# A block-sparse attention and two MLPs on one core: the second MLP's input combinations are made a block ahead, kept in DRAM, and split 768 columns wide

## The chip, the cores and the metric

The kernel runs on one core of a Trainium2 chip. The metric is device time in microseconds (us) of one execution, lower is better. Five engines work side by side, each in the order of its own instructions: PE (matmuls, TensorE), DVE (VectorE), ACT (ScalarE), POOL (GpSimd) and SP (which only issues DMAs here). They wait for each other on semaphores.

## The reference

```python
# attention, 4 batches, 8 heads, 576 positions, 64 channels a head, mask by blocks of 64
scores = where(mask, scale * q @ k.T, -1e9)
x = (softmax(scores) @ v)            # as [2304 tokens, 512 channels]
# first MLP: 512 -> 2048 -> 512
h = x @ w_in;  g = s * relu(h)**2 + b;  x = g @ w_out
# second MLP: 512 -> 2048 -> 512
h = x @ w2_in; g = maximum(0.01 * h, h); out = g @ w2_out
```

All is fp32. The weights come as 64-bit words, which the kernel decodes itself.

## The kernel before

**fp32 out of two halves.** PE multiplies fp32 values rounded to a shorter form (`float32r`). So that nothing is lost, each operand is split: a high part `hi` (a cast on ScalarE) and a low part `lo = x - hi` (a subtraction on VectorE). Each product is three matmuls, hi x hi, hi x lo and lo x hi.

**The first MLP** goes through the tokens in five blocks, with the attention of the next block worked in between. Its result goes channel by token to the DRAM tensor `yT` (line 936), without the constant `c` that b adds; `c_sb` holds c, known only after the fourth block (line 932), and is added when the values are read back. In the first MLP's last stretch the kernel also prepares the second MLP's weights in sixteen "units", each in a tile of the pool `stg` (2 tiles, 16 KB a partition): twelve first, four more (`units(1, ...)`, line 944) in the last block.

**The second MLP** uses a Strassen-Winograd scheme: seven products (`PRODUCTS`, line 387) of 2 x 2 blocks take the place of eight. The tokens go in three blocks `j` of 768 columns, two halves of `NH` = 384; the 2048 hidden channels in two halves. That makes six steps, `STEPS` = (block, half) = (0,0), (0,1), (1,1), (1,0), (2,0), (2,1) on line 962. A step has an input phase, 4 pairs `i` of 7 products (`in_pair`, line 1072, 28 in all), and an output phase, 7 products of 4 pairs each (`out_phase`, line 1113, 28 in all). Every product is six matmuls of 384 columns, on line 1090 or 1156. In both phases the products come in the order `IN_ORDER` = 1, 5, 6, 3, 7, 2, 4. The output phase needs for each of its products a high and a low part of hidden values (`gh2`, 3 tiles, line 1149; `gl2`, 2 tiles, line 1150), VectorE's combinations of the tiles `G` (16 tiles, four a pair), and additions to the results `Y` (4 tiles, line 1168). The second step of a block stores Y to the output.

**The block's input**, `x_load(j)` (line 1011): the four quarters of x (two halves of channels by two halves of tokens, `x11` to `x22`) are read from yT, for the channel chunks c = 0 and c = 1 in turn, as tiles of 384 columns (line 1025); ScalarE adds c (line 1030); VectorE makes the combinations T1 to T4 of Winograd's scheme in place (`comb`, line 1046); and each of the seven operands is split, high part on line 1040, low part on line 1041 (VectorE's subtractions all have line 1003, that of the helper `sub`). The pool `X` has 29 tiles of 384 columns: 28 hold the parts of the current block, so a new block's quarters wait for parts that the last input products give back. A block is used by two steps, and x_load runs three times: at the end of the first MLP, and in the output phases of steps 1 and 3.

**The order of the work** is made by a planner (class `Graph`, line 44). Every piece of work is a step with an engine, an estimated duration, the steps it waits for (`after`), the tiles that it opens and uses, and a due time. `order()` (line 87) plays the schedule through: an engine that is idle takes the ready step with the earliest due time whose tiles are free. A due time only ranks; a step runs early if nothing else is ready. Pools in `inturn` (line 261: stg, X, Y, gl2 and others) give tiles in the order of due times. DMAs are planned one after the other at 300 GB/s. The steps are then emitted in that order, and each engine keeps it. A `gate` (line 77) closes one group of pools and opens another in the same memory once all users of the old one have been placed: `xin` (pool X) takes the attention's place, `mlp2` (pools w2, gh2, gl2, Y, G) that of the first MLP.

**Weights of the second MLP** are loaded a step ahead by `load_units` (line 967): eight input units `wi` (two a pair, 0.92 MB each) and seven output weights `wo` (1.05 MB each), each placed behind the one before (`behind=line[-1:]`). Before, wi and the first four wo sit in the 12 tiles of pool `w`, which the first MLP's weights give back one after the other, and the last three wo in the 3 tiles of `w2`.

Of the kernel before, what the change touches and what calls it, by code (L numbers as in the profile page):

```python
# [8 lines left out]
F32 = mybir.dt.float32  # L9
# [182 lines left out]
NB = 5  # L192
# [4 lines left out]
def kernel(  # L197
# [48 lines left out]
    def close_pools(group):  # L246
        for p in reversed(opened.pop(group)):
            p.release()

    MLP1 = (("stg", 2), ("gh", 2), ("gl", 2), ("g", 1), ("st", 2), ("xh", 4), ("xl", 4))  # L250
    ATT = (("xf", 4), ("k", 2), ("kh", 1), ("kl", 1), ("q", 3), ("qs", 1), ("v", 3), ("p", 2), ("pt", 3), ("sm", 6))
    MLP2 = (("w2", 3), ("gh2", 3), ("gl2", 2), ("Y", 4), ("G", 16))
    XIN = (("X", 29),)
    open_pools("mlp1", "left", MLP1)
    open_pools("att", "right", ATT)
    pools.update({
# [17 lines left out]
    s_sb = const.tile([128, 1], F32, name="s_sb")  # L274
    b_sb = const.tile([128, 1], F32, name="b_sb")
    yT = dr_p.tile([DM, NT], F32, name="yT")
    kept = dr_p.tile([2 * KEEP, 128, 2048], F32, name="kept")
    u_in = dr_p.tile([NF, 128, 2, 896], F32, name="u_in")
    u_out = dr_p.tile([2, 7, 128, 8, 2, 128], F32, name="u_out")
# [675 lines left out]


    G.gate(lambda e: (close_pools("att"), open_pools("xin", "right", XIN)), [k for k, _ in ATT], [k for k, _ in XIN])
    G.gate(lambda e: (close_pools("mlp1"), open_pools("mlp2", "left", MLP2)), [k for k, _ in MLP1], [k for k, _ in MLP2])

    ONE = 6 * (NH / 2400 + 0.013)  # L960
    IN_ORDER = (1, 5, 6, 3, 7, 2, 4)
# [5 lines left out]
    def load_units(n):  # L967

        j, half = STEPS[n]
        if n and STEPS[n - 1][1] == half:  # L970
            for m in (in_w, in_ok):
                for i in range(4):
                    for c in range(2):
                        m[n, i, c] = m[n - 1, i, c]
            for m in (out_w, out_ok):
                for r in range(1, 8):
                    m[n, r] = m[n - 1, r]
            return
        k = 0

        def gate():
            nonlocal k
            k += 1
            return [done[NB - 1, min(NF - 1, KEEP + max(k - 1, -KEEP))]] if n == 0 else []

        for i in range(4):
            for c in range(2):
                w = in_w[n, i, c] = buf("w", [128, 2, 7, 128], F32R, "wi")
                in_ok[n, i, c] = G.add(
                    {"SP": 0.65}, lambda e, w=w, u=8 * half + 2 * i + c: e.dma_start(  # L990
                        out=w().bitcast(F32).rearrange("p s r n -> p s (r n)"), in_=u_in[u]),
                    [*unit_ok[half, 0, i], *gate()], [w], [], t2[n] + 7 * ONE * i - 14, nbytes=917504, behind=line[-1:])
                line.append(in_ok[n, i, c])
        for o, r in enumerate(IN_ORDER):
            w = out_w[n, r] = buf("w2" if r in (7, 2, 4) else "w", [128, 8, 2, 128], F32R, "wo")
            x = OUT7.index(PRODUCTS[r][0])
            out_ok[n, r] = G.add(
                {"SP": 0.65}, lambda e, w=w, half=half, x=x: e.dma_start(out=w().bitcast(F32), in_=u_out[half, x]),
                [*[s for i in range(4) for s in unit_ok[half, 1, i]], *gate()], [w], [], t2[n] + 28 * ONE + 4 * ONE * o - 14, nbytes=1048576, behind=line[-1:])
            line.append(out_ok[n, r])  # L1000
# [5 lines left out]
        return {"DVE": dve(n)}  # L1006

    x2 = {}
    in_last = [None]

    def x_load(j):

        n0 = [n for n, s in enumerate(STEPS) if s[0] == j][0]
        t = t2[n0] - 24
        x2.update({(j, r, c): [buf("X", [128, NH], F32R, "xh2"), buf("X", [128, NH], F32R, "xl2"), None] for r in PRODUCTS for c in range(2)})
        for c in range(2):
            raw, ok = {}, {}
            for a in (1, 2):
                for b in (1, 2):
                    raw[a, b] = buf("X", [128, NH], F32, "xr")  # L1020
                    row, col = (2 * (a - 1) + c) * 128, 2 * NH * j + NH * (b - 1)
                    from_ = [y_st[k, 2 * (a - 1) + c] for k in range(NB) if T0[k] < col + NH and T0[k] + TB[k] > col]
                    t += 0.01
                    ld = G.add(
                        {"SP": 0.65}, lambda e, x=raw[a, b], row=row, col=col: e.dma_start(out=x(), in_=yT[row:row + 128, col:col + NH]),
                        [*from_, in_last[0]], [raw[a, b]], [], t - 4, nbytes=512 * NH)

                    def add_c(e, x=raw[a, b], cc=c_sb[:, 2 * (a - 1) + c:2 * (a - 1) + c + 1]):
                        if e is nc.scalar:
                            e.activation(out=x(), in_=x(), func=ACTF.Identity, bias=cc)  # L1030
                        else:
                            e.tensor_scalar(out=x(), in0=x(), scalar1=cc, scalar2=None, op0=ALU.add)

                    ok[a, b] = G.add({"ACT": act(NH) + 0.05}, add_c, [ld, *c_ok], [], [raw[a, b]], t, port=True)

            def split(r, x, after):
                nonlocal t
                t += 0.6
                hi, lo, _ = x2[j, r, c]
                a = G.add({"ACT": act(NH)}, lambda e: e.activation(out=hi(), in_=x(), func=ACTF.Copy), after, [hi], [x], t)  # L1040
                a = G.add({"DVE": dve(NH)}, lambda e: sub(e, lo(), x(), hi().bitcast(F32)), [a], [lo], [hi, x], t, port=True)
                x2[j, r, c][2] = a
                return a

            def comb(x, y, z, after):
                return G.add(tt(NH), lambda e: sub(e, x(), y(), z()), after, [], [x, y, z], t, port=True)

            x11, x12, x21, x22 = raw[1, 1], raw[1, 2], raw[2, 1], raw[2, 2]
            a = split(1, x11, [ok[1, 1]])
            t1 = comb(x11, x12, x11, [a, ok[1, 2]])  # L1050
            a = split(5, x11, [t1])
            tt2 = comb(x11, x22, x11, [a, ok[2, 2]])
            split(6, x11, [tt2])
            a = split(2, x21, [ok[2, 1]])
            t4 = comb(x21, x21, x11, [a, tt2])
            t3 = comb(x12, x22, x12, [t1, ok[2, 2]])
            split(7, x12, [t3])
            split(4, x21, [t4])
            split(3, x22, [ok[2, 2]])

    gt = {}

# [9 lines left out]
    def in_pair(n, i):  # L1072
# [8 lines left out]
        for o, r in enumerate(IN_ORDER):  # L1081
            due = t + o * ONE
            x, first = where[r]
            ai = IN7.index(PRODUCTS[r][0])

            def fn(e, r=r, x=x, first=first, ai=ai):
                for c in range(2):
                    hi, lo, _ = x2[j, r, c]
                    for m, (s, y) in enumerate(((0, hi), (0, lo), (1, hi))):
                        e.matmul(out=x()[:, :NH], lhsT=in_w[n, i, c]()[:, s, ai], rhs=y(), start=(first and c == 0 and m == 0), stop=(c == 1 and m == 2),  # L1090
                                 skip_group_check=True)

            after = [*[in_ok[n, i, c] for c in range(2)], *[x2[j, r, c][2] for c in range(2)]]
            after += {6: [ev.get(1)], 7: [ev.get(6)], 4: [ev.get(7)], 3: [ev.get(5)]}.get(r, [])
            p = G.add({"PE": ONE}, fn, after, [x] * first, [x, *[in_w[n, i, c] for c in range(2)], *[q for c in range(2) for q in x2[j, r, c][:2]]], due)
            in_last[0] = p
            d2 = due + ONE
            if r in (1, 5, 6):
                y = g[{1: (1, 1), 5: (2, 2), 6: (1, 2)}[r]]
                ev[r] = G.add({"ACT": act(NH)}, lambda e, x=x, y=y: copy(e, y(), x()[:, :NH]), [p], [y], [x], d2)  # L1100
            elif r in (2, 3, 7):
                y = g[{2: (1, 1), 3: (1, 2), 7: (2, 2)}[r]]
                ev[r] = a = G.add({"DVE": dve(NH)}, lambda e, x=x, y=y: add(e, y(), x()[:, :NH]), [p, ev[{2: 1, 3: 6, 7: 5}[r]]], [], [x, y], d2)
                ok[{2: (1, 1), 3: (1, 2), 7: (2, 2)}[r]] = G.add(
                    {"ACT": act(NH)}, lambda e, y=y: e.activation(out=y(), in_=y(), func=ACTF.Lrelu), [a], [], [y], d2 + 2)  # L1105
            else:
                y = g[2, 1]
                ok[2, 1] = G.add({"ACT": act(NH)}, lambda e, x=x, y=y: e.activation(out=y(), in_=x()[:, :NH], func=ACTF.Lrelu), [p], [y], [x], d2)
# [81 lines left out]
    for n in range(len(STEPS)):  # L1190
        if n == 0 or STEPS[n][0] != STEPS[n - 1][0]:
            x_load(STEPS[n][0])
        load_units(n)
        for i in range(4):
            in_pair(n, i)
        out_phase(n)
# [53 lines left out]
```

## Time and profile before

| | |
|---|---|
| median of 3 runs | 967.18 us (963.68 to 967.64) |
| the profiled execution | 969.23 us |
| its span, first to last instruction | 967.2 us |
| PE busy | 940.6 us, 97% |
| VectorE busy | 655.7 us, 68% |
| ScalarE busy | 579.3 us, 60% |
| GpSimd busy | 103.6 us, 11% |
| DMA | 197.26 MB, mean 204 GB/s |

The span lies inside the execution; some 2 us lie around it. Busy times are shares of the whole span; stages differ, and a hole in PE's row counts only where it is. Matmuls overlap in the records: a matmul of 384 columns lasts 335 ns there, while the next one starts some 174 ns after it.

### The profile page before, as it was taken

To read this page: it belongs to the slowest core of one execution; us is meant where nothing else is said; L and a number is where in the kernel's file an instruction comes from. 1 tells how busy PE (TensorE), PEld (TensorE's weight loads), DVE (VectorE), ACT (ScalarE), POOL (GpSimd) and SP (SyncE) were. 2 spreads that over 40 slices of the span, in tenths; PEclk is the share of its full clock that TensorE was granted. 3 is DMA by queue.
4 is the path that set the end of the run, shared out by engine and by line. 5 is a ranking of instruction groups with operands and counts; after the bars stand their busy time and mean duration, and the time that the engine had idled before them with its cause. 6 is when DMAs were issued, how large, how long until landed. Compare 5 with 4: busy or idle time off the path is not lost. (4 is left out here: it accounts for less than half of the span.)

```text
span 967.2 us, 16689 instructions
## 1 busy us (share of the span) xinstructions
PE 940.6 (97%) x5780; PEld 826.7 (85%) x5780; DVE 655.7 (68%) x1342; ACT 579.3 (60%) x1247; POOL 103.6 (11%) x232
## 2 busy tenths in 40 slices
PE   9799999999998999999999999999989999899998
PEld 8678887777776787888887888999989999799998
DVE  5798877777786776676677752556595565955657
ACT  4678666676676566666676632555565555645443
POOL 1112321111121212112221000000000000000000
PEclk9999999999999999999999999999999999999999
DMA  8896277985768987466346996973115741157402
GB/s 221 289 335 205 69 249 258 319 260 194 215 202 244 312 276 246 154 217 189 99 141 186 353 350 218 387 291 139 58 37 199 289 160 57 33 188 288 168 1 66
DMA packets 143828, 197.26 MB, mean 204 GB/s; under 512 B 23296, under 2 KB 118144, under 8 KB 137088
## 3 DMA queue, kind: packets, MB, share of 16 engines
q1 hardware_dynamic: 141296, 195.41, 61.4%
q10 hardware_dynamic: 2448, 0.79, 0.4%
q8 instruction: 46, 0.75, 0.3%
q14 instruction: 38, 0.31, 0.1%
HBM read 148.96 MB, written 47.19 MB: 203 GB/s over the span
## 5 line engine op out<-in xcount | busy, mean ns | idle before, releaser
L874 PE MATMUL h<-xh,w 128*128 128x512 f32 (+1 forms) x640 | 231.7, 392 | 2.6 <-ACT g L890 0.8
L917 PE MATMUL y<-gh,w 128*128 128x512 f32 (+1 forms) x640 | 186.2, 374 | 0.0
L874 PEld LDWEIGHTS h<-xh,w 128*128 128x128 f32 x640 | 118.9, 190 | 30.5 <-issue 5.3
L917 PEld LDWEIGHTS y<-gh,w 128*128 128x128 f32 x640 | 114.6, 188 | 20.8 <-issue 1.1
L1149 ACT ACTIVATE gh<-G 128x384 fp32r<-128x384 f32 x168 | 86.8, 524 | 59.3 <-PE A L1156 25.4
L1003 DVE TENSOR_TENSOR gl<-G,gh 128x384 fp32r<-128x384 f32 x168 | 92.6, 555 | 43.3 <-PE A L1156 18.7
L874 PE MATMUL h<-xl,w 128*128 128x512 f32 (+1 forms) x320 | 118.9, 372 | 1.0 <-DVE xl L857 1.0
L917 PE MATMUL y<-gl,w 128*128 128x512 f32 (+1 forms) x320 | 118.6, 371 | 1.1 <-DVE gl L893 1.0
L1090 PE MATMUL A<-xh,wi 128*128 128x384 f32 x384 | 112.3, 335 | 0.3 <-ACT G L1065 0.2
L1156 PE MATMUL A<-gh,wo 128*128 128x384 f32 x384 | 98.4, 337 | 1.5 <-ACT gh L1149 1.5
L890 ACT ACTIVATE g<-h 128x512 f32<-128x512 f32 (+1 forms) x80 | 44.4, 555 | 71.1 <-PE h L874 63.1
L1090 PEld LDWEIGHTS A<-xh,wi 128*128 128x128 f32 x384 | 70.6, 188 | 1.0 <-ACT G L1065 1.0
L1156 PEld LDWEIGHTS A<-gh,wo 128*128 128x128 f32 x384 | 69.1, 188 | 2.8 <-ACT gh L1149 2.1
L563 PE MATMUL t<-id_sb,p 128*128 128x128 f32 x400 | 66.0, 279 | 5.3 <-DVE p L533 3.1
L917 PEld LDWEIGHTS y<-gl,w 128*128 128x128 f32 x320 | 60.2, 188 | 12.3 <-DVE gl L893 2.0
L1105 ACT ACTIVATE G<-G 128x384 f32<-128x384 f32 x72 | 37.8, 525 | 51.5 <-DVE G L1070 51.4
L479 ACT ACTIVATE pt<-t 128x512 f32<-128x512 f32 (+2 forms) x84 | 44.3, 530 | 39.5 <-PE t L563 38.2
L563 PEld LDWEIGHTS t<-id_sb,p 128*128 128x128 f32 x400 | 47.9, 141 | 22.6 <-issue 7.1
L874 PEld LDWEIGHTS h<-xl,w 128*128 128x128 f32 x320 | 60.9, 190 | 7.3 <-DVE xl L857 1.3
L1156 PE MATMUL A<-gl,wo 128*128 128x384 f32 x192 | 64.7, 337 | 0.3
L1090 PE MATMUL A<-xl,wi 128*128 128x384 f32 x192 | 64.3, 335 | 0.0
L893 DVE TENSOR_TENSOR gl<-g,gh 128x512 fp32r<-128x512 f32 (+1 forms) x80 | 51.4, 643 | 16.5 <-ACT gh L892 14.1
(124 smaller groups left out, 1859.6 us busy)
## 6 DMA issues: line engine op xcount, KB each, us to landing
wi<-u_in SPq DMA_DIRECT2D x32, 896.0 KB, 6.2
wo<-u_out SPq DMA_DIRECT2D x28, 1024.0 KB, 5.7
w<-kept SPq DMA_DIRECT2D x16, 1024.0 KB, 7.0
u_in<-unit SPq DMA_DIRECT2D x16, 896.0 KB, 5.1
u_out<-unit SPq DMA_DIRECT2D x32, 448.0 KB, 5.4
early<-in_moe_w_in_dram SPq DMA_DIRECT2D x16, 512.0 KB, 6.0
early<-in_moe_w_out_dram SPq DMA_DIRECT2D x16, 512.0 KB, 6.7
kept<-w SPq DMA_DIRECT2D x8, 1024.0 KB, 8.0
```

Source lines behind the costliest of these rows:

```text
L479: e.activation(out=out, in_=in_, func=ACTF.Copy, scale=by)
L563: e.transpose(tb()[:, x * 128:(x + 1) * 128], P()[:, pc:pc + 128], id_sb)
L874: e.matmul(out=h()[:, :T], lhsT=w()[:, wi, c * 128:(c + 1) * 128], rhs=x[blk, c]()[:, :T], start=(c == 0 and n == 0), stop=(c == KD - 1 an ...
L890: a = G.add({"ACT": act(T)}, lambda e: e.activation(out=g()[:, :T], in_=h()[:, :T], func=ACTF.Relu), [prev], [g], [h], due)
L893: lo = G.add({"DVE": dve(T)}, lambda e: e.tensor_tensor(out=gl()[:, :T], in0=g()[:, :T], in1=gh()[:, :T].bitcast(F32), op=ALU.subtract), [ ...
L917: e.matmul(out=y()[:, :W], lhsT=w()[:, wi, d * 128:(d + 1) * 128], rhs=x()[:, :W], start=(pos == 0 and n == 0), stop=(pos == NF - 1 and n ...
L1003: e.tensor_tensor(out=out, in0=x, in1=y, op=ALU.subtract)
L1090: e.matmul(out=x()[:, :NH], lhsT=in_w[n, i, c]()[:, s, ai], rhs=y(), start=(first and c == 0 and m == 0), stop=(c == 1 and m == 2), skip_g ...
L1105: {"ACT": act(NH)}, lambda e, y=y: e.activation(out=y(), in_=y(), func=ACTF.Lrelu), [a], [], [y], d2 + 2)
L1149: hi = G.add({"ACT": act(NH)}, lambda e, gh=gh, x=x: e.activation(out=gh(), in_=x(), func=ACTF.Copy), [a], [gh], [x], due - 2)
L1156: e.matmul(out=z[d]()[:, :NH], lhsT=out_w[n, r]()[:, 2 * i + d, s], rhs=y(), start=(first and i == 0 and m == 0), stop=(i == 3 and m == 2) ...
```

## The change

- The input combinations of blocks 1 and 2 are made by a new function `x_stage`, ahead of `x_load`: quarters of both channel chunks are read at once (tiles of 768 columns, `x_raw`), c is added on ScalarE, 384 columns at a time, T1 to T4 are made 768 columns wide, and all seven operands are stored to a new DRAM tensor `x_dr` as fp32. For block 1 this runs in one tile of `stg`, with due times in the last block of the first MLP; for block 2 in the four tiles of `Y`, with due times in step 2.
- `x_load(1)` and `x_load(2)` only read the seven operands and split them, 768 columns an instruction (`x_part`). Loads no longer wait for the last input product (`in_last` is gone); they wait for the store and for a tile of X.
- Block 0 (`x_first`) still goes from yT to its parts in one go, 768 columns wide.
- X has 15 tiles of 768 columns in place of 29 of 384. `gl2` has 3 tiles in place of 2.
- Input units 5, 6 and 7 use `w2`, and all seven output weights use `w`.

The diff, without the old body of x_load, which stands above:

```diff
--- before.py
+++ after.py
@@ -249,8 +249,8 @@
 
     MLP1 = (("stg", 2), ("gh", 2), ("gl", 2), ("g", 1), ("st", 2), ("xh", 4), ("xl", 4))
     ATT = (("xf", 4), ("k", 2), ("kh", 1), ("kl", 1), ("q", 3), ("qs", 1), ("v", 3), ("p", 2), ("pt", 3), ("sm", 6))
-    MLP2 = (("w2", 3), ("gh2", 3), ("gl2", 2), ("Y", 4), ("G", 16))
-    XIN = (("X", 29),)
+    MLP2 = (("w2", 3), ("gh2", 3), ("gl2", 3), ("Y", 4), ("G", 16))
+    XIN = (("X", 15),)
     open_pools("mlp1", "left", MLP1)
     open_pools("att", "right", ATT)
     pools.update({
@@ -274,6 +274,7 @@
     s_sb = const.tile([128, 1], F32, name="s_sb")
     b_sb = const.tile([128, 1], F32, name="b_sb")
     yT = dr_p.tile([DM, NT], F32, name="yT")
+    x_dr = dr_p.tile([2, 7, 128, 2, NH], F32, name="x_dr")
     kept = dr_p.tile([2 * KEEP, 128, 2048], F32, name="kept")
     u_in = dr_p.tile([NF, 128, 2, 896], F32, name="u_in")
     u_out = dr_p.tile([2, 7, 128, 8, 2, 128], F32, name="u_out")
@@ -955,7 +956,6 @@
 
 
     G.gate(lambda e: (close_pools("att"), open_pools("xin", "right", XIN)), [k for k, _ in ATT], [k for k, _ in XIN])
-    G.gate(lambda e: (close_pools("mlp1"), open_pools("mlp2", "left", MLP2)), [k for k, _ in MLP1], [k for k, _ in MLP2])
 
     ONE = 6 * (NH / 2400 + 0.013)
     IN_ORDER = (1, 5, 6, 3, 7, 2, 4)
@@ -985,14 +985,14 @@
 
         for i in range(4):
             for c in range(2):
-                w = in_w[n, i, c] = buf("w", [128, 2, 7, 128], F32R, "wi")
+                w = in_w[n, i, c] = buf("w2" if 2 * i + c > 4 else "w", [128, 2, 7, 128], F32R, "wi")
                 in_ok[n, i, c] = G.add(
                     {"SP": 0.65}, lambda e, w=w, u=8 * half + 2 * i + c: e.dma_start(
                         out=w().bitcast(F32).rearrange("p s r n -> p s (r n)"), in_=u_in[u]),
                     [*unit_ok[half, 0, i], *gate()], [w], [], t2[n] + 7 * ONE * i - 14, nbytes=917504, behind=line[-1:])
                 line.append(in_ok[n, i, c])
         for o, r in enumerate(IN_ORDER):
-            w = out_w[n, r] = buf("w2" if r in (7, 2, 4) else "w", [128, 8, 2, 128], F32R, "wo")
+            w = out_w[n, r] = buf("w", [128, 8, 2, 128], F32R, "wo")
             x = OUT7.index(PRODUCTS[r][0])
             out_ok[n, r] = G.add(
                 {"SP": 0.65}, lambda e, w=w, half=half, x=x: e.dma_start(out=w().bitcast(F32), in_=u_out[half, x]),
@@ -1006,57 +1006,106 @@
         return {"DVE": dve(n)}
 
     x2 = {}
-    in_last = [None]
+
+    class View:
+
+        def __init__(self, buf, view=lambda x: x):
+            self.buf, self.view = buf, view
+
+        def __call__(self):
+            return self.view(self.buf())
+
+    def x_part(j, r, x, after, t):
+
+        hi, lo, _ = x2[j, r]
+        a = G.add({"ACT": act(2 * NH)}, lambda e: e.activation(out=hi(), in_=x(), func=ACTF.Copy), after, [hi], [x.buf], t)
+        x2[j, r][2] = a = G.add({"DVE": dve(2 * NH)}, lambda e: sub(e, lo(), x(), hi().bitcast(F32)), [a], [lo], [hi, x.buf], t, port=True)
+        return a
+
+    def x_raw(j, key, t, name):
+
+        raw, ok = {}, {}
+        whole = buf("stg", [128, 2, 2, 1024], F32, name) if key == "stg" else None
+        for y, (a, b) in enumerate(((1, 1), (1, 2), (2, 2), (2, 1))):
+            if whole is None:
+                x = View(buf(key, [128, 2, NH], F32, name))
+            else:
+                x = View(whole, lambda w, y=y: w[:, y // 2, y % 2, :2 * NH].rearrange("p (c n) -> p c n", c=2))
+            raw[a, b] = x
+            row, col = 2 * (a - 1) * 128, 2 * NH * j + NH * (b - 1)
+            from_ = [y_st[k, 2 * (a - 1) + c] for k in range(NB) for c in range(2) if T0[k] < col + NH and T0[k] + TB[k] > col]
+            t += 0.01
+            ld = G.add(
+                {"SP": 0.65}, lambda e, x=x, row=row, col=col: e.dma_start(
+                    out=x(), in_=yT[row:row + 256, col:col + NH].rearrange("(c p) n -> p c n", c=2)),
+                from_, [x.buf] if whole is None or not y else [], [x.buf], t, nbytes=1024 * NH)
+            ok[a, b] = [
+                G.add({"ACT": act(NH) + 0.05}, lambda e, x=x, c=c, cc=c_sb[:, 2 * (a - 1) + c:2 * (a - 1) + c + 1]: e.activation(
+                    out=x()[:, c], in_=x()[:, c], func=ACTF.Identity, bias=cc), [ld, *c_ok], [], [x.buf], t + 4)
+                for c in range(2)
+            ]
+        return raw, ok
+
+    def x_comb(x, y, z, after, t):
+        return G.add(tt(2 * NH), lambda e: sub(e, x(), y(), z()), after, [], [x.buf, y.buf, z.buf], t, port=True)
+
+    def x_first():
+
+        t = t2[0] - 24
+        for r in PRODUCTS:
+            x2[0, r] = [buf("X", [128, 2, NH], F32R, "xh2"), buf("X", [128, 2, NH], F32R, "xl2"), None]
+        raw, ok = x_raw(0, "X", t - 4, "xr")
+        x11, x12, x21, x22 = raw[1, 1], raw[1, 2], raw[2, 1], raw[2, 2]
+        a = x_part(0, 1, x11, ok[1, 1], t)
+        t1 = x_comb(x11, x12, x11, [a, *ok[1, 2]], t + 1)
+        a = x_part(0, 5, x11, [t1], t + 2)
+        tt2 = x_comb(x11, x22, x11, [a, *ok[2, 2]], t + 3)
+        x_part(0, 6, x11, [tt2], t + 4)
+        t3 = x_comb(x12, x22, x12, [t1, *ok[2, 2]], t + 5)
+        x_part(0, 7, x12, [t3], t + 6)
+        a = x_part(0, 2, x21, ok[2, 1], t + 7)
+        t4 = x_comb(x21, x21, x11, [a, tt2], t + 8)
+        x_part(0, 4, x21, [t4], t + 9)
+        x_part(0, 3, x22, ok[2, 2], t + 10)
+
+    x_st = {}
+
+    def x_stage(j, key, t):
+
+        raw, ok = x_raw(j, key, t, "xs")
+        x11, x12, x21, x22 = raw[1, 1], raw[1, 2], raw[2, 1], raw[2, 2]
+
+        def store(r, x, after):
+            a = x_st[j, r] = G.add({"SP": 0.65}, lambda e: e.dma_start(out=x_dr[j - 1, r - 1], in_=x()), after, [], [x.buf], t + 6, nbytes=1024 * NH)
+            return a
+
+        s1 = store(1, x11, ok[1, 1])
+        t1 = x_comb(x12, x12, x11, [*ok[1, 1], *ok[1, 2]], t + 6)
+        s5 = store(5, x12, [t1])
+        s3 = store(3, x22, ok[2, 2])
+        tt2 = x_comb(x12, x22, x12, [s5, *ok[2, 2]], t + 6)
+        store(6, x12, [tt2])
+        t3 = x_comb(x11, x12, x11, [s1, tt2], t + 6)
+        store(7, x11, [t3])
+        s2 = store(2, x21, ok[2, 1])
+        t4 = x_comb(x21, x21, x12, [s2, tt2], t + 6)
+        store(4, x21, [t4])
 
     def x_load(j):
 
+        if not j:
+            x_first()
+            return
         n0 = [n for n, s in enumerate(STEPS) if s[0] == j][0]
         t = t2[n0] - 24
-        x2.update({(j, r, c): [buf("X", [128, NH], F32R, "xh2"), buf("X", [128, NH], F32R, "xl2"), None] for r in PRODUCTS for c in range(2)})
...
+        for o, r in enumerate(IN_ORDER):
+            x2[j, r] = [buf("X", [128, 2, NH], F32R, "xh2"), buf("X", [128, 2, NH], F32R, "xl2"), None]
+            x = View(buf("X", [128, 2, NH], F32, "xr"))
+            ld = G.add({"SP": 0.65}, lambda e, r=r, x=x: e.dma_start(out=x(), in_=x_dr[j - 1, r - 1]), [x_st[j, r]], [x.buf], [], t - 4 + 0.1 * o, nbytes=1024 * NH)
+            x_part(j, r, x, [ld], t + o)
+
+    x_stage(1, "stg", begin[NB - 1] + 4)
+    G.gate(lambda e: (close_pools("mlp1"), open_pools("mlp2", "left", MLP2)), [k for k, _ in MLP1], [k for k, _ in MLP2])
 
     gt = {}
 
@@ -1085,15 +1134,14 @@
 
             def fn(e, r=r, x=x, first=first, ai=ai):
                 for c in range(2):
-                    hi, lo, _ = x2[j, r, c]
+                    hi, lo, _ = x2[j, r]
                     for m, (s, y) in enumerate(((0, hi), (0, lo), (1, hi))):
-                        e.matmul(out=x()[:, :NH], lhsT=in_w[n, i, c]()[:, s, ai], rhs=y(), start=(first and c == 0 and m == 0), stop=(c == 1 and m == 2),
+                        e.matmul(out=x()[:, :NH], lhsT=in_w[n, i, c]()[:, s, ai], rhs=y()[:, c], start=(first and c == 0 and m == 0), stop=(c == 1 and m == 2),
                                  skip_group_check=True)
 
-            after = [*[in_ok[n, i, c] for c in range(2)], *[x2[j, r, c][2] for c in range(2)]]
+            after = [*[in_ok[n, i, c] for c in range(2)], x2[j, r][2]]
             after += {6: [ev.get(1)], 7: [ev.get(6)], 4: [ev.get(7)], 3: [ev.get(5)]}.get(r, [])
-            p = G.add({"PE": ONE}, fn, after, [x] * first, [x, *[in_w[n, i, c] for c in range(2)], *[q for c in range(2) for q in x2[j, r, c][:2]]], due)
-            in_last[0] = p
+            p = G.add({"PE": ONE}, fn, after, [x] * first, [x, *[in_w[n, i, c] for c in range(2)], *x2[j, r][:2]], due)
             d2 = due + ONE
             if r in (1, 5, 6):
                 y = g[{1: (1, 1), 5: (2, 2), 6: (1, 2)}[r]]
@@ -1191,6 +1239,8 @@
         if n == 0 or STEPS[n][0] != STEPS[n - 1][0]:
             x_load(STEPS[n][0])
         load_units(n)
+        if n == 2:
+            x_stage(2, "Y", t2[n] + 2)
         for i in range(4):
             in_pair(n, i)
         out_phase(n)
```

## Rows read from the trace of the kernel before

**Rows 1.** The page: its first part (busy us, share of the span, instructions) and the granted clock.

```profile
PE 940.6 (97%) x5780; PEld 826.7 (85%) x5780; DVE 655.7 (68%) x1342; ACT 579.3 (60%) x1247; POOL 103.6 (11%) x232
...
PEclk9999999999999999999999999999999999999999
```

**Rows 2.** Stretches: length, busy us (count) of PE, PEld, DVE, ACT, POOL; clock, DMA, GB/s.

```profile
600.00:620.00 20.00, 19.69 (x108) 18.57 (x107) 10.06 (x18) 11.55 (x22) 0.00 (x0) 1.00 0.95 365
680.00:700.00 20.00, 19.64 (x112) 19.09 (x111) 11.50 (x22) 11.81 (x26) 0.00 (x0) 1.00 0.22 70
680.00:740.00 60.00, 56.21 (x315) 54.05 (x314) 44.77 (x90) 35.48 (x75) 0.00 (x0) 1.00 0.24 81
692.93:724.65 31.72, 27.93 (x151) 25.77 (x151) 29.27 (x62) 22.26 (x47) 0.00 (x0) 1.00 0.09 26
740.00:800.00 60.00, 60.00 (x348) 60.00 (x347) 34.08 (x65) 31.35 (x66) 0.00 (x0) 1.00 0.59 218
800.00:860.00 60.00, 56.23 (x315) 54.07 (x314) 43.10 (x87) 35.61 (x75) 0.00 (x0) 1.00 0.25 80
940.00:960.00 20.00, 19.64 (x112) 19.09 (x111) 17.14 (x36) 9.55 (x19) 0.00 (x0) 1.00 0.15 40
```

**Rows 3.** The chain that ended last: start, us, line, matmuls.

```profile
853.29 1.04 PE A L1090 x6
```

**Rows 4.** PE's timeline: start, us, line, tiles, count, idle time ahead and its releaser.

```profile
521.34 0.50 PE L874 MATMUL h<-xh,w 128*128 128x512 f32 x1 [0.76 <-DVE g L888]
...
603.31 0.39 PE L917 MATMUL y<-gl,w 128*128 128x512 f32 x1
...
611.75 0.51 PE L1156 MATMUL A<-gh,wo 128*128 128x384 f32 x2
...
685.65 0.33 PE L1090 MATMUL A<-xh,wi 128*128 128x384 f32 x1
...
691.89 0.34 PE L1090 MATMUL A<-xh,wi 128*128 128x384 f32 x1
...
707.98 0.44 PE L1156 MATMUL C<-gl,wo 128*128 128x384 f32 x1 [1.54 <-DVE gl L1003]
...
720.71 0.44 PE L1156 MATMUL B<-gl,wo 128*128 128x384 f32 x1 [0.98 <-DVE gl L1003]
```

**Rows 5.** VectorE's timeline in the first block switch.

```profile
706.91 0.55 DVE L1003 TENSOR_TENSOR xl<-xr,xh 128x384 fp32r<-128x384 f32 x1
707.38 0.55 DVE L1003 TENSOR_TENSOR gl<-G,gh 128x384 fp32r<-128x384 f32 x1
```

**Rows 6.** Groups by line and shape: busy us, mean ns | idle ahead, releasers.

```profile
L893 DVE TENSOR_TENSOR gl<-g,gh 128x512 fp32r<-128x512 f32 x64 | 44.1, 690 | 16.5 <-ACT gh L892 14.1 <-PE y L917 2.1
...
L1003 DVE TENSOR_TENSOR xl<-xr,xh 128x384 fp32r<-128x384 f32 x42 | 22.7, 551 | 4.6 <-ACT xh L1040 4.6
...
L334 DVE TENSOR_TENSOR w<-early,w 128x1024 fp32r<-128x1024 f32 x15 | 18.3, 1218 | 1.2 <-ACT w L331 1.2
...
L1040 ACT ACTIVATE xh<-xr 128x384 fp32r<-128x384 f32 x42 | 20.3, 512 | 3.3 <-DVE xr L1003 3.3
...
L1030 ACT ACTIVATE xr<-xr,c_sb 128x384 f32<-128x384 f32 x24 | 13.3, 604 | 0.7 <-DMA xr<-yT 0.7
```

**Rows 7.** ScalarE's timeline at the first switch.

```profile
696.52 2.12 ACT L1030 ACTIVATE xr<-xr,c_sb 128x384 f32<-128x384 f32 x4
```

**Rows 8.** DMA issues: KB each, median us from issue to landing.

```profile
xr<-yT SPq DMA_DIRECT2D x24, 192.0 KB, 3.7
```

**Rows 9.** SP's timeline: DMA issues at the first MLP's end.

```profile
529.20 3.72 SPq L417 DMA_DIRECT2D unit<-in_moe_w_out_dram  x1
...
572.41 1.57 SPq L458 DMA_DIRECT2D u_out<-unit  x2
...
605.07 2.43 SPq L998 DMA_DIRECT2D wo<-u_out  x3
```

More of the change, by code (lines that the diff above doesn't have):

```diff
@@ L1011, in x_load @@
     def x_load(j):
+        if not j:
+            x_first()
+            return
         n0 = [n for n, s in enumerate(STEPS) if s[0] == j][0]
         t = t2[n0] - 24
-        x2.update({(j, r, c): [buf("X", [128, NH], F32R, "xh2"), buf("X", [128, NH], F32R, "xl2"), None] for r in PRODUCTS for c in range(2)})
[L1016 to L1038, printed above, removed]
-                hi, lo, _ = x2[j, r, c]
[L1040 to L1059, printed above, removed]
@@ L1087, in fn @@
                 for c in range(2):
-                    hi, lo, _ = x2[j, r, c]
+                    hi, lo, _ = x2[j, r]
                     for m, (s, y) in enumerate(((0, hi), (0, lo), (1, hi))):
-                        e.matmul(out=x()[:, :NH], lhsT=in_w[n, i, c]()[:, s, ai], rhs=y(), start=(first and c == 0 and m == 0), stop=(c == 1 and m == 2),
+                        e.matmul(out=x()[:, :NH], lhsT=in_w[n, i, c]()[:, s, ai], rhs=y()[:, c], start=(first and c == 0 and m == 0), stop=(c == 1 and m == 2),
                                  skip_group_check=True)
-            after = [*[in_ok[n, i, c] for c in range(2)], *[x2[j, r, c][2] for c in range(2)]]
+            after = [*[in_ok[n, i, c] for c in range(2)], x2[j, r][2]]
             after += {6: [ev.get(1)], 7: [ev.get(6)], 4: [ev.get(7)], 3: [ev.get(5)]}.get(r, [])
-            p = G.add({"PE": ONE}, fn, after, [x] * first, [x, *[in_w[n, i, c] for c in range(2)], *[q for c in range(2) for q in x2[j, r, c][:2]]], due)
-            in_last[0] = p
+            p = G.add({"PE": ONE}, fn, after, [x] * first, [x, *[in_w[n, i, c] for c in range(2)], *x2[j, r][:2]], due)
             d2 = due + ONE
```

## The prediction

> **What bounds the kernel now.** I began with the busy shares: PE is busy 97% of the span with its clock granted in full, VectorE 68% [rows 1]. So only fewer matmuls, which the change doesn't bring, or fewer holes in PE's row can shorten the run. I looked for the holes of the second MLP in its stretches. Undisturbed, 60 us start 348 matmuls; the two stretches from 680 and from 800, in which the tokens of a block give way to the next, start 315 each; the last output phase, which no block follows, starts 112 in 20 us where 116 or 117 belong [rows 2]. A product of six matmuls takes 1.04 us [rows 3], one matmul so 0.1735 us:
>
> - each block switch: 33 x 0.1735 = 5.7 us lost
> - last output phase: some 5 x 0.1735 = 0.9 us lost
>
> An output phase that ends a block so loses 0.9 us of itself; what the preparation of the next block costs is 2 x (5.7 - 0.9) = **9.6 us**, 1% of the time. That is nearly all that this change can reach here.
>
> Who holds PE up stands in PE's timeline: it waits for a low part, `gl`, from VectorE, 1.54 us and 0.98 us in the first switch [rows 4]. VectorE is busy 29.27 of 31.72 us there, with 62 instructions [rows 2], and its timeline shows them nose to tail, one every 0.47 us, the new block's `xl` in line with the `gl` that PE waits for [rows 5]. So VectorE is the bound of these two stretches, by throughput. Elsewhere in the second MLP it isn't: 34.08 of 60 us after the switch [rows 2].
>
> **The change part by part.** *Arithmetic at a switch.* Before, a block costs VectorE 14 splits (`xl`) and 8 combinations (`xr`), 22 instructions of 384 columns, which at 0.47 us are 10.3 us; ScalarE makes 8 additions of c (0.604 us each) and 14 casts (0.512) [rows 6]. Afterwards a switch keeps 7 splits of 768 columns. No such instruction is in the trace; 512 columns take 0.690 us and 1024 take 1.218 [rows 6], so half-way is 0.954. Back to back an instruction hides 0.08 of its 0.55 us behind the next [rows 5], so I charge 0.87: 7 x 0.87 = 6.1 us. VectorE is relieved of 10.3 - 6.1 = **4.2 us** at each switch (by whole durations, without the overlap: 22 x 0.55 - 7 x 0.954 = 5.4). ScalarE loses its additions too, and isn't the bound.
>
> [...]
>
> *When it runs.* Before, the first addition of the new block runs at 696.5 [rows 7]: the planner puts its loads after the last input product, and then follow addition, combination and split, for two halves in turn. Afterwards the seven ready combinations are only loaded, into tiles that the last input products give back one by one. These seven products start between 685.7 and 691.9 [rows 4]; a load lands 3.7 us after its issue [rows 8]. So splits can start near 690, where VectorE is still half idle (11.50 of 20 us [rows 2]). That is an estimate: the planner's new order is in no trace.
>
> The sum for a switch: of VectorE's 62 instructions 40 stay, 40 x 0.47 = 18.8 us, and 6.1 us of splits make 24.9, some of it ahead of the stretch. PE's 150 matmuls in that stretch need 150 x 0.1735 = 26.0 us. VectorE falls from 29.1 us, 112% of PE's need, to 96% or less: no longer the bound, but near enough for single waits, and an instruction of 0.87 us keeps a `gl` waiting longer than one of 0.47. I take 4.3 of the 4.8 us: **-8.6 us** for both. The bounds: 4.2 each if VectorE stays saturated, 4.8 if nothing is left.
>
> *The third `gl` buffer.* VectorE can now run two low parts ahead and falls behind when additions to Y come. Three output phases end a block and lose 0.9 us each: between 0 and 2.7 us. The additions themselves stay, so I take **-0.3**.
>
> *The stage of block 2 (tiles Y, step 2).* New work in another place: 4 loads, 8 additions on ScalarE, 4 combinations of 0.87 = 3.5 us on VectorE, 7 stores. Tiles Y come free as block 0's results are stored, so it may begin at the end of the first switch; the rest falls behind it, where VectorE has 26 of 60 us free [rows 2]. If all of it fell into the saturated stretch, that switch would win 4.2 - 3.5 = 0.7 us. I charge **+0.4**. Its stores wait on SP's queue for VectorE, and the input units of step 3 wait behind them; these are wanted some 50 us later.
>
> *The stage of block 1 (tile stg, last block of the first MLP).* Again 8 x 0.604 = 4.8 us of ScalarE and 3.5 us of VectorE, after c is known, at some 515 to 540. VectorE prepares weights there, and PE waits for it once, 0.76 us [rows 4]. Between 0 and 1.5 us (two more such waits); **+0.5**. The tile also takes one of two stg slots from the last four weight units. Their last stores are issued at 572.4 [rows 9], and the first MLP's matmuls end at 603.5 [rows 4]: some 25 us in hand.
>
> *Weights in other pools.* Three input units now use w2, which is there only once the first MLP's tiles are gone, and all seven output weights queue behind them. Before, just three output weights were loaded after that point, at 605.1 [rows 9]. Afterwards ten transfers start there, 3 x 0.92 + 7 x 1.05 = 10.1 MB. At the 365 GB/s that were moved around then [rows 2], the first output weight, 3.8 MB down the line, comes after 10.4 us and some 2 of landing, at 617.5; the last near 635. Before, PE took its first output product at 611.75 [rows 4]. What can cover the gap is the step's 28 input products, 28 x 1.04 = 29 us, for which the 16 tiles G suffice; the planner has these loads' times and can pull the products ahead. Without that cover PE waits 617.5 - 611.75 = 5.8 us, and some 2 more for the next weights. I charge **+0.4**.
>
> Sum: -8.6 - 0.3 + 0.4 + 0.5 + 0.4 = **-7.6 us**. The profiled execution took 969.23 us (span 967.2) and would take 961.6. The median of the runs, 967.18, is 2.05 us below it; the forecast is **959.6 us**.
>
> **The rivals.** *VectorE stays the bound (0.22, no change).* The splits start no earlier, block 2's stage falls into the first switch, and the three charges double, of which block 2's is then in the 0.7: 4.9 won, 1.8 paid, -3.1, or 964.1. For it speaks that the planner fills any hole with whatever is ready; against it, that it ranks the stage behind the output phase's work.
>
> *Output weights are late (0.08, no change).* PE is sent to the output products as early as before: -8.0 without my charge, + 7.8 = -0.2, or 967.0. Against it: the order is made anew, with the loads' times in it.
>
> *The stage holds stg too long (0.08, slower).* The last four units begin to load at 529.2 [rows 9] and take some 50 us over two slots, 25 us of a slot each. If the stage keeps its slot until they are through, they need 4 x 25 us in the other and end at 629; G, Y and w2 wait for that, and PE with them, 25 us: -7.6 + 25, or 984.6. It decides once the stage holds its slot for about 50 us (four units and the stage in 2 x 74 us of slots up to 603). I work its chain out as 3.7 us of load, 4.8 of additions, three combinations and two stores between them, at a landing like the load's: some 20 us. Not very likely, therefore.
>
> **How the numbers follow.** My case has 0.62. Its own range is 955.5 to 962: at the low end all 9.6 us of the switches, 2.1 of the third buffer's 2.7 and no charge. The high end, 967.0, takes in the first two rivals; the last one, and the scatter of runs at the ends (963.68 to 967.64 before), are the less than 2 in 10 left out. A difference under 0.5%, 4.8 us, can't be told from none here. Faster by more: my case and a little of the first rival, 0.64. Within: most of the first, the second and a little of mine, 0.26. Slower: the last and some unforeseen stall of the new order, 0.10.
>
> **What would show it.** Right: the stretches from 680 and 800 (now earlier by what was won) start over 335 matmuls in 60 us; VectorE idles again in them; splits take about 0.95 us and begin before the last input product; the stage of block 2 lies behind the switch. Wrong: waits for `gl` of over a microsecond remain there; PE idles between 605 and 620 for output weights; or the last unit is stored later than 603.

## The result, and the profile after

The changed kernel takes 956.89 us (median of 4 runs, 954.47 to 958.44), the kernel before 967.41 beside it; the ratio is 0.9891 with a 95% interval of 0.9849 to 0.9933. The forecast was 959.6 us, 955.5 to 967.0. The profiled execution has a span of 956.6 us in place of 967.2.

Stretches of the changed kernel, in the columns of [rows 2] and for the same times, except that the last output phase, which begins some ten us earlier now, is read from 920 to 940:

```profile
600.00:620.00 20.00, 19.66 (x109) 18.55 (x108) 8.94 (x16) 11.89 (x23) 0.00 (x0) 1.00 0.93 362
...
680.00:740.00 60.00, 59.54 (x344) 59.08 (x343) 44.82 (x81) 37.12 (x73) 0.00 (x0) 1.00 0.52 176
...
800.00:860.00 60.00, 59.54 (x343) 59.08 (x343) 41.83 (x79) 33.13 (x65) 0.00 (x0) 1.00 0.37 128
920.00:940.00 20.00, 19.70 (x114) 19.38 (x114) 12.99 (x27) 9.65 (x19) 0.00 (x0) 1.00 0.00 1
```

The two switches start 344 and 343 matmuls where they started 315 [rows 2]: (29 + 28) x 0.1735 us = 9.9 us. VectorE's busy time from 680 to 740 is nearly the same as before, 44.82 against 44.77 us, because three of the four combinations of block 2's stage lie in there now and PE gets further into the next step; yet PE hardly waits. What counts is what stands in VectorE's queue between the `gl`, not the sum over 60 us.

PE's timeline after: these three waits are all that is left at the output phases (in [rows 4] VectorE's `gl` held PE up by 1.54 and 0.98 us):

```profile
699.42 0.62 PE L1204 MATMUL A<-gh,wo 128*128 128x384 f32 x2 [0.46 <-DVE Y L1119]
...
816.78 0.61 PE L1204 MATMUL A<-gh,wo 128*128 128x384 f32 x2 [0.46 <-DVE Y L1119]
...
932.42 0.62 PE L1204 MATMUL A<-gh,wo 128*128 128x384 f32 x2 [0.30 <-DVE Y L1119]
```

VectorE's timeline at the first switch, with the first and the last of its seven splits:

```profile
691.13 0.95 DVE L1003 TENSOR_TENSOR xl<-xr,xh 128x768 fp32r<-128x768 f32 x1
...
702.48 0.95 DVE L1003 TENSOR_TENSOR xl<-xr,xh 128x768 fp32r<-128x768 f32 x1
703.35 0.55 DVE L1003 TENSOR_TENSOR gl<-G,gh 128x384 fp32r<-128x384 f32 x1
703.82 0.95 DVE L1003 TENSOR_TENSOR xl<-xr,xh 128x768 fp32r<-128x768 f32 x1
...
722.15 1.07 DVE L1119 TENSOR_TENSOR Y<-A,Y 128x384 f32<-128x384 f32 x2 [2.66 <-PE A L1204]
...
724.25 0.95 DVE L1003 TENSOR_TENSOR xs<-xs 128x768 f32<-128x768 f32 x1
```

The splits begin before the last input product and are through by 704.8; before, the first addition alone came at 696.5 [rows 7]. In a full queue a split takes 703.35 - 702.48 = 0.87 us, as charged. VectorE idles 2.66 us towards the end of the switch, and the first combination of block 2's stage (`xs`) comes behind that.

### The profile page after: what moved, and what is told of

It reads as the page before. It is cut to its first block, busy times and chain, and to the rows that moved or that the text cites. A ratio compares the mean times of both kernels' runs of the same rounds, so it can differ in the third digit from the quotient of the medians.

```text
span 956.6 us, 16663 instructions
## 1 busy us (share of the span) xinstructions
PE 938.8 (98%) x5780; PEld 828.4 (87%) x5780; DVE 651.8 (68%) x1308; ACT 577.1 (60%) x1227; POOL 101.4 (11%) x232
## 4 chain that ended last, share of the span: by engine, by line
PE 87%; DVE 2%; DMA 2%; ACT 1%; issue 1%; SPq 1%; POOL 0%; DVEq 0%; ACTq 0%; POOLq 0%
PE h L875 19%; PE y L918 19%; PE A L1204 10%; PE A L1139 10%; PE C L1139 5%; PE C L1204 5%; PE o L826 4%; PE t L564 4%; PE B L1204 3%; PE B L1139 3%; PE s L747 2%; PE s L787 1%; PE s L549 1%; DMA k<-in_k_dram 1%; DMA q<-in_q_dram 0%
## 5 line engine op out<-in xcount | busy, mean ns | idle before, releaser
L480 ACT ACTIVATE pt<-t 128x512 f32<-128x512 f32 (+2 forms) x80 | 42.0, 527 | 35.6 <-PE t L564 34.0
```

The source lines that it names most:

```text
L480: e.activation(out=out, in_=in_, func=ACTF.Copy, scale=by)
```

## The experiments

The total time carries the first MLP's scatter: in the profiled executions its last matmul starts at 597.6 us in e10, at 601.0 in e0 and at 603.3 in the kernel before, though these three differ only in what comes behind it. So beside the total each experiment has the length of its second MLP, from the start of the first MLP's last matmul to the start of the last matmul of all. For the two kernels these are, in PE's timeline (before, where the first of the two rows is the one at 603.31 in [rows 4]; then after):

```profile
963.17 0.34 PE L1156 MATMUL A<-gl,wo 128*128 128x384 f32 x1
```

```profile
602.90 0.39 PE L918 MATMUL y<-gl,w 128*128 128x512 f32 x1
...
952.64 0.34 PE L1204 MATMUL A<-gl,wo 128*128 128x384 f32 x1
```

359.9 and 349.7 us: 10.1 of the 10.6 us that the profiled spans differ by. Each length in the table comes from one profiled execution, and how much it scatters was not measured, so differences of about 1 us between two rows carry little. Each ratio is to the runs of the kernel before that were made beside that kernel's own (medians from 966.74 to 967.64 us).

| kernel | median, us | ratio to before (95%) | second MLP, us |
|---|---|---|---|
| before | 967.41 | | 359.9 |
| changed | 956.89 | 0.9891 (0.9849 to 0.9933) | 349.7 |
| e0_no_prep | 954.71 | 0.9880 (0.9849 to 0.9910) | 348.6 |
| e1_wide_at_switch | 960.71 | 0.9949 (0.9929 to 0.9969) | 355.5 |
| e2_staged_narrow | 958.23 | 0.9920 (0.9895 to 0.9945) | 350.8 |
| e5_loads_late | 960.18 | 0.9923 (0.9894 to 0.9952) | 352.3 |
| e3_gl2_two | 960.31 | 0.9923 (0.9901 to 0.9945) | 351.9 |
| e4_before_pools_gl2 | 966.49 | 0.9991 (0.9975 to 1.0007) | 358.8 |
| e8_low_twice | 968.34 | 1.0005 (0.9990 to 1.0021) | 359.5 |
| e9_wide_late | 965.79 | 0.9991 (0.9972 to 1.0011) | 359.7 |
| e10_before_early | 966.38 | 0.9984 (0.9966 to 1.0002) | 360.5 |
| e7_hold_1 | 959.68 | 0.9916 (0.9892 to 0.9940) | 350.8 |
| e7_hold_2 | 976.51 | 1.0093 (1.0067 to 1.0119) | 364.3 |
| e11_y_first | 957.46 | 0.9903 (0.9875 to 0.9931) | 349.1 |

The theory is the prediction's: VectorE's work at the two switches holds PE up, and the change takes enough of it away. The rivals: the gain comes from wider instructions as such, from the earlier start, or from the third `gl` buffer and the new pools.

**What is there to win (e0_no_prep).** The kernel before, without any preparation of blocks 1 and 2.

```diff
     def x_load(j):
+        if j:
+            x2.update({(j, r, c): x2[0, r, c] for r in PRODUCTS for c in range(2)})
+            return
```

> The kernel before, with the preparation of blocks 1 and 2 left out (loads, additions of c, combinations, splits): their products use block 0's operands, so two thirds of the output are not the reference's. If VectorE's load at the two block switches is what the change took away, the switches lose about 0.9 us each in place of 5.7 and the run takes about 967.4 - 9.6 = 957.8 us, within 1 us of the changed kernel. If the gain comes from the third gl buffer, the weights' pools or the new order of the first MLP, which are all as before here, it stays above 963.

954.71 us and a second MLP of 348.6: with the preparation gone, 11.3 us are, where 9.6 were expected. Pools, buffers and all else are as before, so the cause lies in that work. The changed kernel, which still does its splits there, comes within 1.1 us of it. This run takes away work of ScalarE and loads too; the next one touches VectorE alone.

**Putting the load back (e8_low_twice).** The changed kernel, with each low part of blocks 1 and 2 computed twice.

```diff
         x2[j, r][2] = a = G.add({"DVE": dve(2 * NH)}, lambda e: sub(e, lo(), ...
+        if j:
+            x2[j, r][2] = a = G.add({"DVE": dve(2 * NH)}, lambda e: sub(e, lo(), ...), [a], [], [lo, hi, x.buf], t, port=True)
```

> The changed kernel with the low part of every split of blocks 1 and 2 computed twice (the second one writes the same values): 7 x 0.87 = 6.1 us more of VectorE at a switch, which then has 12.2, more than the 10.3 of the kernel before. If VectorE's throughput there is the bound: 2 to 4 us a switch come back, 961 to 965 us, with waits for gl. If only the early start or the waits in the chain counted: 957 to 958.

The whole gain is gone (359.5 us), more than was expected, with stages, early loads, width and third buffer all in place. Its load at a switch is 12.2 us against 10.3 before the change. PE's timeline of this kernel at the first switch:

```profile
701.11 1.01 PE L1206 MATMUL A<-gh,wo 128*128 128x384 f32 x2 [2.13 <-DVE Y L1121]
...
712.03 0.44 PE L1206 MATMUL C<-gl,wo 128*128 128x384 f32 x1 [0.95 <-DVE gl L1003]
```

Two matmuls take 1.01 us behind that wait of 2.13, where two take 0.62 behind the waits above: the granted clock was 0.75 from 700 to 702 and 0.50 from 702 to 704, of which more below. PE's waits in the second MLP grow from 1.5 to 7.0 us, which is 5.5 of the 9.8 us that are lost; the lower clock in both switches (0.97 on the mean from 680 to 740 and from 800 to 860, where the changed kernel has 1.00) is the likely rest. The waits were expected for `gl`; 5.0 of the 7.0 us are for additions to Y, which stand in the same queue of VectorE.

**The parts: width and the stage (e1, e2, e9).** e1 prepares all blocks as block 0 is; e9 is e1 with the loads planned late and two gl buffers, so that little but the width is left; e2 keeps the stages and halves the splits' width.

```diff
-    def x_first():
+    def x_first(j):            # e1: for every block; both calls of x_stage are gone
...
-                from_, ...
+                [*from_, in_last[0]], ...                      # e9 besides, and ("gl2", 2)
...
+            for c in range(2):                                 # e2, in x_part for j > 0
+                a = G.add({"ACT": act(NH)}, ... hi()[:, c] ...)
+                x2[j, r][2] = a = G.add({"DVE": dve(NH)}, ... lo()[:, c] ...)
```

> The changed kernel without the stages: every block is prepared at its switch as block 0 is, 768 columns wide, early loads kept. VectorE has 11 wide instructions at a switch, 11 x 0.87 = 9.6 us in place of 10.3 before and 6.1 in the changed kernel. If moving the combinations a block ahead is what counts: part of the loss stays, 1.5 to 4 us a switch, 960 to 964 us. If width (fewer instructions) or the early start is what counts: 957 to 958.

> No stages, loads planned behind the last input product, two gl buffers, but 768 columns wide: of the change only the width (and the weights' pools) is left. VectorE's 11 wide instructions are 9.6 us in place of 10.3. If throughput at the switch is the bound: 0.7 us a switch, 965 to 967 us, the second MLP (last matmul of the first MLP to last matmul) 357.5 to 359.9 us where the kernel before takes 359.9. If fewer, wider instructions are the gain: 960 or less.

> The changed kernel with the splits of blocks 1 and 2 in halves of 384 columns: 14 x 0.47 = 6.6 us of VectorE at a switch in place of 6.1. If the combinations' move counts and width little: 957 to 959 us. If width counts: 961 or more.

Width with the new pools is worth 0.1 us of the second MLP (e9), and some 1.1 us are lost when the staged splits are narrow (e2), as 0.5 us of VectorE a switch would have it. With everything except the stages, 4.4 us are won (e1); the stages bring the other 5.7. So the combinations' and additions' move out of the switch is the largest part, and the width counts for little.

The 0.1 us of e9 is a net result. PE's waits for `gl` in the second MLP did fall, from 6.2 to 4.5 us, which is about what 0.7 us of VectorE a switch should give; but its waits for ScalarE rose from 1.7 to 3.1 us. In each switch ScalarE waits for a combination (`xr`) of VectorE, and a copy into G that PE needs stands behind the casts of 768 columns that follow. ScalarE's timeline of e9, and PE's:

```profile
704.19 0.85 ACT L1022 ACTIVATE xh<-xr 128x768 fp32r<-128x768 f32 x1 [1.41 <-DVE xr L1003]
...
707.65 0.47 ACT L1113 ACTIVATE G<-A 128x384 f32<-128x384 f32 x1
```

```profile
708.17 0.44 PE L1138 MATMUL A<-xh,wi 128*128 128x384 f32 x1 [1.45 <-ACT G L1113]
```

**The parts: the start (e5, e10).** The changed kernel with late loads, and the kernel before with early ones.

```diff
-... [x_st[j, r]], [x.buf], [], t - 4 + 0.1 * o, ...
+... [x_st[j, r], in_last[0]], [x.buf], [], t - 4 + 0.1 * o, ...   # e5
...
-... [*from_, in_last[0]], [raw[a, b]], ...
+... from_, [raw[a, b]], ...                                       # e10
```

> The changed kernel with the loads of blocks 1 and 2 planned behind the last input product again, as before the change. VectorE's load is that of the changed kernel, 24.9 us where PE needs 26.0, but all of it lies in the stretch after 693. If throughput is what counts: at most 1.5 us a switch is lost again, 957 to 960 us. If the early start is what counts: 962 or more.

> The kernel before with one thing changed: its loads no longer wait in the plan for the last input product. All 22 narrow instructions stay at the switch. If spare time of VectorE ahead of the stretch is worth what the late loads cost the changed kernel (2.4 us of its second MLP): 963 to 966 us, second MLP 356 to 359. If the early start alone were the gain: 959 or less. If quarters find no free tile before the last input products anyway: 967.

e5 loses 2.5 us, 1.3 a switch: its first split comes at 695.2 in place of 691.1. e10 missed its expectation: the first split came ten microseconds earlier (689.1 in place of 699.6), yet its second MLP took 360.5 us, no less than before. Its waits in the second MLP did shrink, from 7.9 to 6.3 us in total, but they gathered in one place of each switch, 1.84 us for the additions to Y at the start of product 6, and the granted clock fell behind it. PE's timeline of e10, and two stretches of it in the columns of [rows 2]:

```profile
694.08 0.62 PE L1156 MATMUL A<-gh,wo 128*128 128x384 f32 x2 [1.84 <-DVE Y L1070]
...
696.13 0.84 PE L1156 MATMUL A<-gh,wo 128*128 128x384 f32 x2
696.77 0.53 PE L1156 MATMUL A<-gl,wo 128*128 128x384 f32 x1
697.09 0.84 PE L1156 MATMUL A<-gh,wo 128*128 128x384 f32 x2
```

```profile
694.00:696.00 2.00, 1.78 (x6) 1.47 (x7) 2.00 (x6) 0.52 (x2) 0.00 (x0) 0.75 0.00 0
696.00:698.00 2.00, 2.00 (x8) 2.00 (x7) 2.00 (x5) 0.94 (x2) 0.00 (x0) 0.50 0.00 0
```

So the early start by itself won nothing in the kernel before. With the smaller load of the changed kernel it is worth 2.5 us; which of the other changes it needs was not separated.

**The parts: buffers and pools (e3, e4).** The changed kernel with two `gl` tiles; the kernel before with three and with the new places of the weights.

```diff
-... ("gl2", 3), ...
+... ("gl2", 2), ...                                              # e3
...
-... ("gl2", 2), ("Y", 4), ...
+... ("gl2", 3), ("Y", 4), ...                                    # e4, and both buf() lines of load_units as in the change
```

> The changed kernel with two gl buffers as before. If the switches' relief is the gain: 957 to 959.5 us (0 to 0.9 us at each of three output phases). If the third buffer is the gain: 964 or more.

> The kernel before with only the third gl buffer and the new places of the weights (input units 5 to 7 in w2, output weights in w). If VectorE's preparation work at the switches is the cause: 965 to 967.5 us, since at a VectorE that has no spare time a further buffer brings nothing. If buffers are the gain: 957 to 960. If late output weights cost anything, it shows here as PE idle between 605 and 625.

The third buffer is worth 2.1 us in the changed kernel; its total, 960.31 us, lies between the two expected cases, so it is neither nothing nor the gain itself. With the pools it brings 1.1 us in the kernel before, where the total can't be told from no change. The late output weights cost nothing (below).

What each part costs when it is taken out of the changed kernel, 5.7 (stages), 2.5 (start), 2.1 (buffer) and 1.1 us (width of the splits), adds up to 11.4, more than the 10.1 that all of them bring: the parts overlap.

**The case on the other side (e7).** The changed kernel, with the last store of block 1's stage waiting for a weight unit, 13 in the one and 14 in the other, so that the stage keeps its stg tile.

```diff
-        store(4, x21, [t4])
+        store(4, x21, [t4, *(unit_ok[1, 1, 1] if j == 1 else [])])   # e7_hold_1; [1, 1, 2] in e7_hold_2
```

> The changed kernel with block 1's stage keeping its stg tile until weight unit 13 is stored (its last store waits for that). In the changed kernel the last unit's stores are issued at 598, so hardly 5 us before the first MLP's tiles have to be given up. If that is the edge past which the second MLP's start is held up: the last unit ends 7 to 20 us later and PE idles as long around 605 to 625, 962 to 975 us. If the order absorbs it: 957 to 958.

> The changed kernel, block 1's stage keeping its stg tile until weight unit 14 is stored. Keeping it until unit 13 moved the last unit's low part from 594.2 to 600.9 us and held nothing up. Now units 12 to 14 must pass through the other tile one by one: the last unit should end 10 to 25 us later, past the end of the first MLP's matmuls at 603. If that is the edge, PE idles 8 to 25 us between 603 and 630 and the run takes 965 to 982 us. If the planner again absorbs it: 957 to 960.

The first holds up nothing at the start of the second MLP, though its last unit is split at 600.9 only: its expectation missed, since the planner had let units 14 and 15 run side by side. The second is slower than the kernel before. One stretch of it, its PE, its SP and its ScalarE:

```profile
600.00:620.00 20.00, 11.76 (x51) 10.69 (x50) 10.04 (x13) 8.35 (x11) 0.00 (x0) 0.75 0.54 177
```

```profile
615.76 0.69 PE L1139 MATMUL A<-xh,wi 128*128 128x384 f32 x1 [8.24 <-ACT G L1114]
...
625.54 0.44 PE L1139 MATMUL A<-xh,wi 128*128 128x384 f32 x1 [3.24 <-DVE G L1119]
```

```profile
615.36 3.77 SPq L459 DMA_DIRECT2D u_out<-unit  x4
```

```profile
613.63 1.70 ACT L448 ACTIVATE unit<-unit 128x1792 fp32r<-128x1792 f32 x1 [2.94 <-DVE unit L442]
615.24 0.47 ACT L1114 ACTIVATE G<-A 128x384 f32<-128x384 f32 x1
...
623.90 0.52 ACT L1197 ACTIVATE gh<-G 128x384 fp32r<-128x384 f32 x1 [5.11 <-DMA u_out<-unit]
```

The last unit is cast at 613.6 and stored from 615.4 on, and what the second MLP puts into the first MLP's memory stands behind it. ScalarE's first copy into G follows that cast, and PE's first wait, 8.24 us, ends with it. ScalarE's first `gh` waits 5.11 us for the unit's stores; VectorE's `gl` and, behind it in its queue, the next addition to G follow, and PE's second wait, 3.24 us, ends with that. Together PE stands idle for 11.5 us.

**The rest of the waits (e11_y_first).** The changed kernel with the additions to Y of product 1 due earlier.

```diff
-... [p, prev], [], [y, z[d]], due + ONE)
+... [p, prev], [], [y, z[d]], due - 8 * (o == 0))
```

> The changed kernel with an earlier due time for VectorE's two additions of product 1 to Y in steps 1, 3 and 5, for which PE waits 0.46, 0.46 and 0.30 us there. If these waits and the slow restart behind them are the rest of the loss, 0.5 to 0.8 us each of three: second MLP 347.5 to 349 us where the changed kernel takes 349.7, the run 954.5 to 957. If others take their place: 956 to 958.

The three waits for Y are gone and none takes their place: of PE's waits in the second MLP only one of 0.2 us is left, and its length falls by 0.6 us in all, to 349.1, where 0.5 to 0.8 us for each of the three were expected. The total doesn't show it (957.46 us). None of the runs that compute the reference's output clearly beats the changed kernel.

## Why the prediction was right, point by point

- **The bound: right.** e0 and e8 show it from both sides. The 9.6 us put on the preparation were 11.3 by e0.
- **The arithmetic: right.** 7 splits at 0.952 us (0.954 was estimated), 0.87 in a full queue. Width itself is worth little (e9, e2), as it should by the working's own prices: 11 instructions of 768 columns in place of 22 of 384 make 0.7 of the 4.2 us.
- **When it runs: right.** Splits start at 691.1 ("near 690"). e5 sizes it: 1.3 us a switch.
- **The sum of the switches, -8.6, and the third buffer, -0.3: right in kind, small by 1.** 9.9 us came back at the switches. The mis-sized term is the buffer: by e3 it carries 2.1 us, near the upper end of its bounds (0 to 2.7). That a third tile pays once VectorE has idle time, and little before (1.1 us with the pools, e4), is the likely reading. Without the buffer, everything else won 8.0 us (e3). So the 7.6 us of the forecast became 10.1 in the second MLP: 1.8 more for the buffer, 1.3 for charges that didn't show, 0.6 less for the switches.
- **The three charges, +1.3 in sum: not seen,** though half a microsecond in the first MLP could not be seen in its scatter. Block 2's stage stands behind the switch, its first combination at 724.3, and the 20 us from 720 start 118 matmuls. In the last block of the first MLP PE's wait of 0.76 us [rows 4] is gone. The late weights were covered as argued: SP issues the three input units at 604.4 and the output weights from 605.9 (it was 605.1 for the last three, [rows 9]). The first output weight lands 10.6 us after its issue, at 616.5 (617.5 was estimated, with "some 2 of landing"; in the kernel before a load of 192 KB from yT took 2.4 us at the least and 3.7 in the median). PE takes its first output product at 621.7 in place of 611.75 [rows 4], and starts 109 matmuls from 600 to 620 where it started 108 [rows 2].
- **The slower rival: the margin was misread, and that it didn't come was in part luck.** "Some 25 us in hand" shrank to about 5: the last unit's last stores, issued at 572.4 before [rows 9], are now issued at 596.2 with the first MLP ending at 602.9. The row at 529.2 [rows 9], from which the rival counts four units, is that of the last two; the first two are loaded together at 490. SP's timeline before, then after:

```profile
490.25 6.15 SPq L417 DMA_DIRECT2D unit<-in_moe_w_out_dram  x8
```

```profile
422.87 1.82 SPq L1039 DMA_DIRECT2D xs<-yT  x3
...
490.88 2.54 SPq L418 DMA_DIRECT2D unit<-in_moe_w_out_dram  x4
...
528.40 2.62 SPq L418 DMA_DIRECT2D unit<-in_moe_w_out_dram  x4
...
535.27 0.32 SPq L1079 DMA_DIRECT2D x_dr<-xs  x1
...
596.23 1.68 SPq L459 DMA_DIRECT2D u_out<-unit  x2
```

The chain itself is as short as estimated (first addition at 514.6, last store at 535.3). But the tile is taken at 422.9: a step runs when its tile is free, not when it is due, and c comes only from 513.1 on. So stg had one tile less for the units for 112 us, not for 20. Of these, 45 us fall behind 490, when the last four units want both tiles: close to the 50 us at which the rival was to decide. The rows show what it did: a unit has four loads, so one unit is loaded at 490 where it was two, the second comes 38 us later, and the last stores 24 us later. That a longer hold ends in a stall is shown too (e7_hold_2).

## What to carry to other kernels

Where a helper engine is the bound for 30 us (VectorE busy 29.27 of 31.72 us, [rows 2]) and has nearly half its time free for the next 90 (busy 49.58 of the 90.54 us from 724.65 in the kernel before), moving a part of its work a stage ahead, at the price of a trip through DRAM, was worth nearly the whole loss here (10.1 of 11.3 us, with the third buffer), while making the same work a little cheaper in place won almost nothing (0.1 us, e9). Count the instructions that stand in its queue between those that the main engine waits for; its busy time over a longer stretch stayed the same here (44.77 and 44.82 of 60 us). And when a prefetch is given a tile of a shared pool, look for when it takes the tile, not for when it is due.

## What the runs showed of the hardware

- In three runs a wait of PE had a lower granted clock with it or behind it, and cost more than its length. In e10 PE waited 1.84 us, and from 696 to 698 the granted clock was 0.50: one matmul of 384 columns each 0.32 us in place of 0.174 (three from 696.13 to 697.09). In e8, behind the wait of 2.13 us, it was 0.75 from 700 to 702 and 0.50 from 702 to 704, and in e7_hold_2 it was 0.50 from 612 to 620, from within the wait of 8.24 us on; in the kernel before, 1.00 was granted in the stretch with its wait of 1.54 us [rows 2, 4].
- A two-tensor operation of 768 columns in fp32 on VectorE took 0.952 us (mean of 21 splits, changed kernel) and one of 384 took 0.551 [rows 6]; in a full queue one started 0.87 and 0.47 us after the other. The overlap was 0.08 us at both widths (0.952 - 0.87 and 0.551 - 0.47).
- The DMAs moved 418 GB/s from 620 to 640 in the changed kernel, while PE started 116 matmuls: loads from DRAM, the rest of the three input units and seven output weights (10.1 MB, issued from 604.4 to 612.2), and the input units behind them (issued from 614.0 on).
